# A new priority order in an attention and two-MLP kernel: the first weight group loaded ahead of the first values

## The chip, the cores and the metric

The kernel runs on one core of a Trainium2 chip. The metric is the time of one execution on the device in microseconds, median of the runs shown. Engines: PE (matrix products), DVE (vector), ACT (scalar and activation), POOL, and SP, which here only issues DMAs.

## The reference

Three steps follow one another on 2 images of 576 tokens, 8 heads of 64: attention, a first MLP, and a sum of four experts.

```python
scores = scale * np.matmul(q, k.transpose(0, 1, 3, 2))
mask_local = (rel >= 0) & (rel < stride)               # heads 0 to 3
mask_strided = (rel >= 0) & (pos[None, :] % stride == pos[:, None] % stride)   # heads 4 to 7
scores = np.where(masks[None, :, :, :], scores, -1000000000.0)
attn = softmax(scores)                                 # row maximum taken away
x = (attn @ v), heads side by side                     # 1152 x 512
h = np.maximum(np.maximum(x @ w1, x @ w2), x @ w3)     # 512 -> 768
x = h @ w_out                                          # 768 -> 512
p = domain_probs / (domain_probs.sum(-1, keepdims=True) + 1e-09)
for e in range(4):
    out += p[:, e:e + 1] * (np.maximum(x @ w1[e], 0.0) @ w2[e])   # 512 -> 1024 -> 512
```

The weights of the first MLP arrive as 64-bit floats, all else as 32-bit.

## The kernel before

Tokens are worked on in four parts i = 0 to 3: image i // 2, and in it the first 256 tokens (i even) or the last 320 (i odd). Heads go in four pairs p: 0 and 1 are the local ones, 2 and 3 the strided ones. Matrix products behind the attention use two 16-bit halves of each operand (a high and a low part, three products each), so every operand is scaled by a power of two and split: ACT writes the high half, DVE the low half (`split`, L135 to L137).

The attention and the first MLP are written as small steps ("atoms"), named by two letters and one or two digits; the string `ORDER` (L37) lists them, and the loop at L634 emits them one after another. The emission order is a priority: the framework (`schedule_with_timeline_sim`, L853) lays out a fixed order for each engine in advance from it, from data dependencies and free buffers, with times of its own. On the chip each engine then runs its list in that order. A wait of one instruction therefore holds what stands behind it on that engine.

The atoms:

- `lq i p` (L202) loads queries and keys of a part and pair, `lv i kind` (L208) its values (kind 0 local, 1 strided); `lw g` (L357) loads weight group g of the first MLP (one sixth of its hidden columns, all three matrices), `lo` (L429) half of its output matrix. All are DMAs issued by SP. Weight groups and output halves alternate between two landing buffers (`st64`, L66).
- `aa i p` (L233): scores on PE (a mask product at L259, then L264), row maximum on DVE (L268), its negative on DVE or POOL, exponentials with row sums on ACT (L275). `an` (L287): division by the sum on POOL and DVE. `at` (L300): transposes on PE (L310), copy on ACT (L312). `ap` (L315): product with the values (L337), then the scaled split into x (L344 on ACT, L345 on DVE).
- `vs i` (L222): scale of the values: two absolute maxima on DVE (L132), a maximum over partitions by a product on PE (L98, "rows") and a DVE reduction (L100), then small DVE steps to a power of two and its reciprocal (L105). Every scale goes through this chain (`scale_of`, `scale_of64`).
- `wd g` (L156): decoding of 64-bit words: two steps on ACT (L162, L163), two on DVE (L166, L167); the second writes tile r, of which there is one buffer (`RB`). `wa g` (L363): scale of a group, and `wp g` (L376): its split. `wa` has two branches: if the group is not yet decoded it takes a maximum over the raw words on DVE, else a sum of absolute values over the decoded ones on ACT (L129).
- `g i g'` (L382, digits part and group): 36 products into three PSUM tiles, combined by ACT, DVE and POOL (L396 to L400). `go i c` (L405): the second product of the first MLP, evicted by ACT (L418).
- `oa`, `od`, `os`, `op`: the same preparation for the output matrix. `fo` closes the attention's buffers and `cl` those of the first MLP.
- `ew`, `fw` (one step each of `prep_w1(0)`, L503, and `prep_w2(0)`, L533): the first expert's weights: a load, eight sums on ACT (L129), a scale, then splits; 17 steps of `ew` in all, of which the 11th to 17th are splits. `xw`, `yw` (`x2_ops`, L459): operands of the first expert's input for even and odd parts, 8 steps each. `m` (`gemm1(0, 0)`, L553): one of four blocks of the first expert's first product, seven products each, summed by DVE (L572 to L579).

The experts follow in a loop (L714). After each block of products a "slot" runs some steps of the next weights' preparation; `XS`, `W20`, `W10`, `W2S` and `W1S` (L31 to L35) say how many.

Of the kernel before, what the change touches and what calls it, by code (L numbers as in the profile page):

```python
# [27 lines left out]
ARS = 'pppd'  # L28
RB = 1
QB = 3  # L30
XS = [0, 0, 2]  # L31
W20 = [0, 1, 1, 2, 1, 5, 1, 2]
W10 = [4, 1, 2, 2, 5, 0, 4, 0]
W2S = [0, 1, 0, 0, 1, 1, 4, 4, 3, 0, 7, 5, 7, 3, 0, 3, 1]
W1S = [9, 3, 1, 2, 0, 13, 6, 6, 4, 0, 4, 4, 0, 6, 0, 4, 2]  # L35

ORDER = """  # L37
    lq00 aa00 lv01 lq03 lv00 lq01 aa01 vs0 an00 lq02 at00 ap00 lq20 aa02 lv21 lw0 an01 at01 ap01 an02 at02
    ap02 lw1 lq22 aa03 an03 at03 wa0 lq21 lq23 wd0 ap03 lv20 aa20 vs2 wa1 lq10 aa21 wd1 wp0 an20 at20 ap20
    lq12 lw3 an21 at21 aa22 g00 aa23 ap21 wp1 an22 lw2 lv11 at22 ap22 g01 wa2 an23 at23 lv10 lq11 ap23 wd2 wa3  # L40
    wd3 wp3 aa11 wp2 g20 lq32 g21 lv30 g03 aa10 an11 aa12 g23 vs1 lw4 at11 ap11 an10 at10 ap10 wa4 wd4 g02 wp4
    lq13 an12 lq30 g04 lv31 aa13 at12 ap12 lw5 wa5 an13 at13 lo0 lq31 wd5 lq33 wp5 aa30 ap13 g22 aa33 aa31 vs3
    lo1 an30 g24 at30 ap30 an31 at31 an33 ap31 at33 ap33 g25 aa32 an32 at32 ap32 oa0 od0 oa1 od1 os fo op0 ew
    g05 op1 op2 g10 op3 ew op4 ew op5 ew go20 ew go00 ew go23 ew g11 ew go22 ew g12 ew go21 ew go01 ew ew go03
    ew go02 g13 ew xw ew fw xw xw g14 ew g15 xw xw xw xw g30 g31 xw xw g32 g34 fw fw g33 fw fw g35 cl go10 m
    fw go13 m go30 fw go11 go12 fw go31 go32 go33 m yw m yw yw yw yw yw yw yw yw
"""
TINY = 2.0**-100
REBIAS = 2.0**-112
# [4 lines left out]
def kernel(ctx, tc, qk0l, qk0s, qk1l, qk1s, vl, vs0, vs1, vn, masks, w123, wo, probs, we1, we2, out):  # L54
# [652 lines left out]
    def step(gen, n=1):  # L707
        for _ in range(n):
            if gen is not None:
                next(gen, None)  # L710
# [3 lines left out]
    for e in range(E):  # L714
# [4 lines left out]
        def slot(k):  # L719
            nonlocal early  # L720
            if e == 0 and k < 8:
                step(gens["w2"], XS[k - 4] if k < 7 else 40)
            if k < 8 and e:
                step(w2g[e - 1], W2S[k] if k < 7 else 40)
            elif more:
                step(w2g[e], (W20 if k < 8 else W2S)[k])
            if more:
                n = 40 if k == 16 else W10[k] if e == 0 and k < 8 else W1S[k]
                if k < 8:
# [127 lines left out]
```

## Time and profile before

| | |
|---|---|
| time, median of 3 runs | 584.34 us (583.85 to 585.56) |
| the profiled execution's own time | 585.75 us |
| its span, first to last instruction | 584.0 us |
| mean granted TensorE clock | 0.974 |
| PE busy | 555.5 us (95%) |
| DVE busy | 367.5 us (63%) |
| ACT busy | 262.4 us (45%) |
| POOL busy | 125.9 us (22%) |
| DMA moved | 44.33 MB |

Shares over the whole span hide that the stages differ: the attention and the first weights lie in the first sixth or so, the experts in the last 350 us. The table of 40 slices and the table by stage are to be read first. PE's granted clock is a share of its full 2.4 GHz; the other level is half of it, and a number between is a mean over a stretch.

### The profile page before, as it was taken

Reading aid. Unit: us, or ns where it says so; the run is one execution under the profiler, and the core shown is the slowest. Engines: PE = TensorE matmul, PEld = TensorE weight load, DVE = VectorE, ACT = ScalarE, POOL = GpSimd, SP = SyncE. Lnnn points to the kernel's source line nnn. Section 1 sums busy time; section 2 is a strip of 40 time slices with the busy share of each in tenths; the row PEclk is TensorE's granted clock in tenths of the full one; section 3 lists DMA queues with packets and bytes.
Section 4 is the critical chain, followed back from the end, with each engine's and each line's share of the span. In section 5 each row is a group of like instructions: output and inputs, shape, how many; then the busy total and the mean of one; then the engine's idle time right before and its main releaser. Section 6 shows DMA issues by size and latency. Waiting matters only on the chain.

```text
span 584.0 us, 9782 instructions
## 1 busy us (share of the span) xinstructions
PE 555.5 (95%) x3943; PEld 375.7 (64%) x3943; DVE 367.5 (63%) x677; ACT 262.4 (45%) x557; POOL 125.9 (22%) x115
## 2 busy tenths in 40 slices
PE   7787889999799999999999999999999999999997
PEld 5576668888677777765445875445876445876443
DVE  4889799763773253888774865893765943765111
ACT  3868679573662122638654533523443520443000
POOL 1234344320212101012424221250221200221000
PEclk9679889999999999999999999999999999999999
DMA  8997355200040002203161000151000000000111
GB/s 274 389 304 253 142 192 192 88 2 1 2 145 0 1 2 74 73 1 121 36 230 47 1 2 1 39 184 65 2 1 1 1 0 1 1 2 0 55 54 55
DMA packets 16109, 44.33 MB, mean 76 GB/s; under 512 B 2280, under 2 KB 2280, under 8 KB 15296
## 3 DMA queue, kind: packets, MB, share of 16 engines
q1 hardware_dynamic: 15920, 43.41, 22.0%
q8 instruction: 31, 0.51, 0.4%
q10 hardware_dynamic: 144, 0.30, 0.2%
q14 instruction: 14, 0.11, 0.1%
HBM read 41.34 MB, written 2.36 MB: 75 GB/s over the span
## 4 chain that ended last, share of the span: by engine, by line
PE 82%; DVE 6%; ACT 4%; DMA 4%; issue 2%; POOL 1%; SPq 0%; DVEq 0%; ACTq 0%
PE e L350 11%; PE e L352 11%; PE e L351 10%; PE w L564 8%; PE w L566 8%; PE w L565 8%; PE g L350 7%; PE g L351 7%; PE g L352 7%; DMA v<-in_vs_dram 3%; PE ops L337 1%; PE sps L264 1%; DMA qk<-in_qk0l_dram 1%; ACT w1ops L136 1%; DVE r L167 1%
## 5 line engine op out<-in xcount | busy, mean ns | idle before, releaser
L565 PE MATMUL w<-xops,w1ops 128*128 128x256 f16 (+1 forms) x448 | 128.0, 286 | 0.7 <-DVE xops L473 0.7
L564 PE MATMUL w<-xops,w1ops 128*128 128x256 f16 (+1 forms) x448 | 127.6, 286 | 1.0 <-DVE c L573 0.6
L566 PE MATMUL w<-xops,w1ops 128*128 128x256 f16 (+1 forms) x448 | 128.0, 286 | 0.0
L350 PE MATMUL g<-x,w 128*128 128x256 f16 (+1 forms) x288 | 83.1, 291 | 4.2 <-ACT t L396 2.9
L351 PE MATMUL g<-x,w 128*128 128x256 f16 (+1 forms) x288 | 83.8, 292 | 0.0
L352 PE MATMUL g<-x,w 128*128 128x256 f16 (+1 forms) x288 | 83.0, 290 | 0.0
L586 POOL TENSOR_TENSOR h<-c,h 128x640 f16<-128x640 f32 (+1 forms) x28 | 36.5, 1303 | 185.6 <-ACT h L585 181.3
L694 DVE SCALAR_TENSOR_TENSOR x2acc<-e,coef,x2acc 128x512 f32<-128x512 f32 x27 | 20.1, 747 | 69.5 <-PE e L352 69.5
L588 ACT ACTIVATE h<-c 128x512 f16<-128x512 f32 (+1 forms) x36 | 24.1, 676 | 83.4 <-DVE c L578 83.2
L352 PE MATMUL e<-w,h 128*128 128x512 f16 x144 | 54.6, 379 | 0.0
L350 PE MATMUL e<-st,h 128*128 128x512 f16 x144 | 54.6, 379 | 0.0
L351 PE MATMUL e<-st,h 128*128 128x512 f16 x144 | 54.6, 379 | 0.0
L352 PE MATMUL e<-st,h 128*128 128x512 f16 x144 | 54.6, 379 | 0.0
L351 PE MATMUL e<-w,h 128*128 128x512 f16 x144 | 54.4, 379 | 0.0
L350 PE MATMUL e<-w,h 128*128 128x512 f16 x144 | 54.0, 379 | 0.0
L565 PEld LDWEIGHTS <-w1ops 128*128 128x128 f16 x448 | 43.8, 98 | 13.4 <-issue 1.6
L566 PEld LDWEIGHTS <-w1ops 128*128 128x128 f16 x448 | 43.8, 98 | 12.6 <-issue 1.7
L564 PEld LDWEIGHTS <-w1ops 128*128 128x128 f16 x448 | 43.8, 98 | 11.9 <-DVE c L577 0.2
L352 PEld LDWEIGHTS <-h 128*128 128x128 f16 x288 | 28.2, 98 | 34.0
L350 PEld LDWEIGHTS <-h 128*128 128x128 f16 x288 | 28.2, 98 | 33.0
L351 PEld LDWEIGHTS <-h 128*128 128x128 f16 x288 | 28.2, 98 | 32.7
L400 POOL TENSOR_TENSOR h<-t,h 128x256 f16<-128x256 f32 (+1 forms) x24 | 24.9, 1040 | 96.8 <-ACT h L399 96.8
(128 smaller groups left out, 1029.0 us busy)
## 6 DMA issues: line engine op xcount, KB each, us to landing
st<-in_we_dram SPq DMA_DIRECT2D x16, 1024.0 KB, 5.4
st<-in_w_dram SPq DMA_DIRECT2D x6, 1536.0 KB, 12.1
st<-in_wo_dram SPq DMA_DIRECT2D x2, 1536.0 KB, 6.4
qk<-in_qk1s_dram SPq DMA_DIRECT2D x4, 684.0 KB, 11.2
out_dram<-x2acc SPq DMA_DIRECT2D x8, 256.0 KB, 2.0
qk<-in_qk1l_dram SPq DMA_DIRECT2D x4, 496.0 KB, 11.4
qk<-in_qk0l_dram SPq DMA_DIRECT2D x4, 400.0 KB, 7.5
qk<-in_qk0s_dram SPq DMA_DIRECT2D x4, 384.0 KB, 11.1
```

Source lines behind the costliest of these rows:

```text
L136: nc.scalar.activation(hi, src, AF.Copy, scale=s)
L167: nc.vector.scalar_tensor_tensor(ri, gi, 3, lw, ALU.logical_shift_left, ALU.bitwise_or)
L350: nc.tensor.matmul(psum, lh, rh, start=i == 0, stop=False)
L351: nc.tensor.matmul(psum, lh, rl, start=False, stop=False)
L352: nc.tensor.matmul(psum, ll, rh, start=False, stop=i == n - 1)
L400: nc.gpsimd.tensor_tensor(hh[:, 1, fc, :], t1[:, :n], hh[:, 0, fc, :], ALU.subtract)
L564: nc.tensor.matmul(pt, wh, xh, start=k == 0, stop=False)
L565: nc.tensor.matmul(pt, wh, xl, start=False, stop=False)
L566: nc.tensor.matmul(pt, wl, xh, start=False, stop=k == 1)
L586: nc.gpsimd.tensor_tensor(lo, c[:, b], hi, ALU.subtract)
L588: nc.scalar.activation(hi, c[:, b], AF.Relu)
L694: nc.vector.scalar_tensor_tensor(acc[:, t, :], pt, coef[:, t : t + 1], acc[:, t, :], ALU.mult, ALU.add)
```

## The change

The atoms and their number stay the same; their order changes, and the slot counts with it. At the start `lq02` comes first and `lw0` ahead of `lv01`, `lq03` and `lv00`; `wa0`, `wd0` and `wp0` (scale, decoding and split of group 0) come ahead of the divisions, transposes and value products of part 0; `wa1` and `wd1` come behind part 0 and the first scores of part 2. `wd2` now stands ahead of `wa2`. Later on, `oa1` and `op3` are moved ahead of `oa0` and `op0`, the steps `ew`, `fw`, `xw` are dealt out anew among the `go` and `g1` blocks (the 15th to 17th `ew` now stand behind `g14`, `g33` and two more `xw`), and the last `m` stands behind eight `yw` in place of one.

```diff
--- before.py
+++ after.py
@@ -28,22 +28,22 @@
 ARS = 'pppd'
 RB = 1
 QB = 3
-XS = [0, 0, 2]
-W20 = [0, 1, 1, 2, 1, 5, 1, 2]
-W10 = [4, 1, 2, 2, 5, 0, 4, 0]
-W2S = [0, 1, 0, 0, 1, 1, 4, 4, 3, 0, 7, 5, 7, 3, 0, 3, 1]
-W1S = [9, 3, 1, 2, 0, 13, 6, 6, 4, 0, 4, 4, 0, 6, 0, 4, 2]
+XS = [0, 1, 1]
+W20 = [2, 1, 3, 2, 0, 5, 1, 2]
+W10 = [1, 1, 2, 2, 4, 4, 0, 3]
+W2S = [0, 0, 1, 0, 1, 1, 4, 6, 3, 0, 7, 5, 7, 3, 1, 3, 1]
+W1S = [8, 3, 1, 2, 0, 14, 6, 6, 4, 0, 4, 4, 0, 5, 0, 3, 3]
 
 ORDER = """
-    lq00 aa00 lv01 lq03 lv00 lq01 aa01 vs0 an00 lq02 at00 ap00 lq20 aa02 lv21 lw0 an01 at01 ap01 an02 at02
-    ap02 lw1 lq22 aa03 an03 at03 wa0 lq21 lq23 wd0 ap03 lv20 aa20 vs2 wa1 lq10 aa21 wd1 wp0 an20 at20 ap20
-    lq12 lw3 an21 at21 aa22 g00 aa23 ap21 wp1 an22 lw2 lv11 at22 ap22 g01 wa2 an23 at23 lv10 lq11 ap23 wd2 wa3
-    wd3 wp3 aa11 wp2 g20 lq32 g21 lv30 g03 aa10 an11 aa12 g23 vs1 lw4 at11 ap11 an10 at10 ap10 wa4 wd4 g02 wp4
-    lq13 an12 lq30 g04 lv31 aa13 at12 ap12 lw5 wa5 an13 at13 lo0 lq31 wd5 lq33 wp5 aa30 ap13 g22 aa33 aa31 vs3
-    lo1 an30 g24 at30 ap30 an31 at31 an33 ap31 at33 ap33 g25 aa32 an32 at32 ap32 oa0 od0 oa1 od1 os fo op0 ew
-    g05 op1 op2 g10 op3 ew op4 ew op5 ew go20 ew go00 ew go23 ew g11 ew go22 ew g12 ew go21 ew go01 ew ew go03
-    ew go02 g13 ew xw ew fw xw xw g14 ew g15 xw xw xw xw g30 g31 xw xw g32 g34 fw fw g33 fw fw g35 cl go10 m
-    fw go13 m go30 fw go11 go12 fw go31 go32 go33 m yw m yw yw yw yw yw yw yw yw
+    lq02 lq00 lq01 aa00 lw0 lv01 lq03 lv00 aa01 vs0 wa0 wd0 an00 lq20 at00 ap00 lw1 aa02 lv21 wp0 an01 at01
+    ap01 an02 lq22 aa03 an03 at02 lv20 ap02 at03 lq21 lq23 ap03 aa20 vs2 lq10 aa21 wa1 an20 at20 wd1 ap20 lq12
+    aa22 g00 lw3 an21 at21 aa23 ap21 wp1 an22 lw2 lv11 at22 ap22 an23 g01 at23 lv10 lq11 ap23 wd2 wa2 wa3 wd3
+    wp3 aa11 wp2 g20 lq32 g21 lv30 an11 g03 aa10 g23 aa12 vs1 lw4 at11 ap11 an10 at10 ap10 lq30 wa4 wd4 lq13
+    wp4 g04 g02 an12 lv31 aa13 at12 ap12 lw5 wa5 an13 at13 wd5 lq33 wp5 aa30 an30 ap13 lo0 lq31 aa33 aa31 vs3
+    g22 lo1 g24 at30 ap30 an31 at31 an33 oa1 at33 ap31 ap33 aa32 an32 oa0 at32 g25 od0 od1 ap32 os op3 op0 g10
+    op4 fo ew g05 op1 op2 ew ew op5 go20 ew go00 ew go23 ew ew g11 ew ew go22 ew g12 go21 ew go01 ew go03 ew
+    go02 ew xw g15 xw g13 fw g14 ew xw xw g30 g31 xw g32 xw fw g33 ew xw xw ew xw g34 fw fw fw g35 cl go10 m
+    go11 go30 fw m go13 fw go12 go31 go32 go33 m yw yw yw yw yw yw yw yw m yw fw
 """
 TINY = 2.0**-100
 REBIAS = 2.0**-112
```

## Rows read from the trace of the kernel before

**Rows 1.** Page, part 2: busy tenths in 40 slices of 14.6 us

```profile
PE   7787889999799999999999999999999999999997
DVE  4889799763773253888774865893765943765111
```

**Rows 2.** Busy us by stage: PE, PEld, DVE, ACT, POOL; clock, DMA share, GB/s

```profile
0.00:80.00 80.00, 60.55 (x496) 48.15 (x497) 61.80 (x116) 53.14 (x162) 25.08 (x40) 0.83 0.79 269
10.00:20.00 10.00, 9.06 (x57) 7.53 (x58) 7.05 (x23) 8.17 (x44) 3.83 (x9) 0.59 1.03 388
80.00:150.00 70.00, 70.00 (x705) 58.87 (x703) 50.20 (x98) 43.03 (x107) 17.77 (x23) 1.00 0.23 77
150.00:162.00 12.00, 8.78 (x65) 6.99 (x64) 10.78 (x11) 10.02 (x14) 4.48 (x3) 0.86 0.03 5
162.00:235.00 73.00, 73.00 (x558) 54.29 (x556) 29.47 (x63) 24.28 (x55) 9.19 (x10) 1.00 0.14 44
235.00:252.00 17.00, 15.43 (x123) 11.62 (x121) 16.88 (x39) 8.36 (x15) 0.00 (x0) 1.00 0.18 63
252.00:584.00 332.00, 327.79 (x2005) 195.77 (x2004) 198.35 (x355) 123.62 (x205) 69.34 (x40) 1.00 0.12 40
```

**Rows 3.** DMA issues, as in part 6 of the page: KB, us to landing

```profile
st<-in_w_dram SPq DMA_DIRECT2D x6, 1536.0 KB, 12.1
v<-in_vl_dram SPq DMA_DIRECT2D x2, 384.0 KB, 11.1
qk<-in_qk0l_dram SPq DMA_DIRECT2D x4, 400.0 KB, 7.5
qk<-in_qk0s_dram SPq DMA_DIRECT2D x4, 384.0 KB, 11.1
v<-in_vs_dram SPq DMA_DIRECT2D x2, 256.0 KB, 7.0
```

**Rows 4.** Instructions in order of time, start and us; values, group 0, part 0

```profile
9.58 1.22 DVE L132 TENSOR_REDUCE vm<-v 96x1 f32<-96x1024 f32 x1 [1.57 <-DMA v<-in_vl_dram]
...
10.97 0.34 ACT L275 ACTIVATE p<-sps,anm 128x96 f32<-128x96 f32 x1 [8.31 <-DVE anm L272]
...
13.71 0.15 DVE L105 RECIPROCAL s<-inv 128x1 f32<-128x1 f32 x1
...
18.10 1.72 DVE L132 TENSOR_REDUCE mx<-st 128x1 bf16<-128x1536 f32 x1
...
18.85 0.49 ACT L344 ACTIVATE x<-ops,s 128x256 f16<-128x256 f32 x1
...
37.59 0.45 DVE L345 SCALAR_TENSOR_TENSOR x<-ops,s,x 128x256 f16<-128x256 f32 x1
```

**Rows 5.** Instructions grouped by line and shape: busy us, mean ns, idle before

```profile
L132 DVE TENSOR_REDUCE mx<-st 128x1 bf16<-128x1536 f32 x6 | 10.4, 1741 | 1.1 <-DMA st<-in_w_dram 1.1
L166 DVE SCALAR_TENSOR_TENSOR st<-st 128x1536 int32<-128x1536 int32 x8 | 16.1, 2017 | 0.7 <-ACT st L163 0.4
L167 DVE SCALAR_TENSOR_TENSOR r<-st 128x1536 int32<-128x1536 int32 x6 | 11.2, 1864 | 0.0
L129 ACT ACTIVATE w1ops<-st 128x512 f16<-128x512 f32 x8 | 4.9, 614 | 0.0
```

**Rows 6.** Instructions in order of time, PE, its longest stall

```profile
31.52 0.29 PE L98 MATMUL rows<-identb,red 128*128 128x128 bf16 x1 [4.42 <-DVE red L95]
```

**Rows 7.** Instructions in order of time, DVE: group 2's maximum, scale, low half

```profile
43.02 1.75 DVE L132 TENSOR_REDUCE mx<-st 128x1 bf16<-128x1536 f32 x1 [1.11 <-DMA st<-in_w_dram]
...
61.09 0.15 DVE L105 RECIPROCAL s<-sinv 128x1 f32<-128x1 f32 x1
...
65.85 1.80 DVE L137 SCALAR_TENSOR_TENSOR w<-r,s,w 128x1536 f16<-128x1536 f32 x1
```

**Rows 8.** Instructions in order of time, ACT and PE, at 150 us

```profile
150.04 6.34 ACT L136 ACTIVATE w1ops<-st,s 128x1024 f16<-128x1024 f32 x6 [4.08 <-DVE s L105]
...
157.88 0.27 PE L350 MATMUL g<-h,wo_t 128*128 128x256 f16 x1 [3.22 <-ACT x2acc L418]
```

## The prediction

> **What bounds the kernel now.** I read the page's table of 40 slices first [rows 1]. The reader is to see two regimes in the PE line: sevens and eights in the first six slices (to about 88 us), then nines to the end, with a single seven in slice 11 (146 to 161 us) and the tail. DVE shows seven to nine tenths in slices 2 to 8 and falls off behind them. The table by stage [rows 2] puts numbers on it. From 0 to 80 us PE is busy for 60.55 us, so 19.45 us are idle, and DMA is busy 0.79 of the time; DVE works 61.80 us there. From 80 to 150 and from 162 to 235 us PE is never idle. Between them, from 150 to 162 us, it loses 3.22 us of idle time, and the granted clock averages 0.86, which over 12 us is another 1.7 us lost. From 235 to 252 us it loses 1.57 us with DVE busy for 16.88 of 17 us. After 252 us PE is idle for 4.2 us, nearly all of it the tail in which the last results are written out.
>
> So everything behind 80 us is PE work at full clock, in a queue. What the change makes of the end is decided by how much of that work is done, or startable, before 80 us, and by the two holes. A microsecond gained anywhere behind 80 us by an engine other than PE is worth nothing unless it closes a hole.
>
> **The moved load.** The change puts the load of weight group 0 (lw0) ahead of the first values (lv01, lv00) and of lq03, and lq02 ahead of everything. All of them are issues of SP; I take them to land in the order of issue. Sizes are in [rows 3]; in 10 to 20 us the queue moves 388 GB/s [rows 2]. Before, the first local values (lv00) end behind 400 + 256 + 384 + 384 KB and DVE's reduction over them starts at 9.58 us, on their arrival [rows 4]. After, 384 + 400 + 400 + 1536 + 256 + 384 KB are ahead of them: 3360 against 1040 KB, 2320 KB more, 6.1 us at 388 GB/s, so about 15.7 us. Group 0 itself has 1184 KB ahead of it in place of 2864 KB: 1680 KB less, 4.4 us, so its reduction can start at about 13.7 instead of 18.10 us [rows 4].
>
> What the late values cost: the scale of the values must be ready before the first x of image part 0 is written, at 18.85 us on ACT [rows 4]. From the reduction's start at 9.58 us to the end of the reciprocal at 13.86 us the chain took 4.3 us. At that length the scale is there at 20.0 us, and the first x comes 1.2 us later than before. What the early group gains: before, the four x of part 0 are complete at 38.04 us by the last line of [rows 4], and by then DVE has also spent the reduction and the two decoding steps of group 1, 1.74 + 2.02 + 1.86 = 5.6 us by their means [rows 5]. In the new order wa1 and wd1 stand behind the whole of part 0 (behind ap03, aa20, vs2). So x of part 0 can be complete 5.6 - 1.2 = 4.4 us earlier, with group 0 ready for it. PE's longest stall of all, 4.42 us before the row at 31.52 us, is a value-scale product that waits for a small DVE reduction [rows 6], queued among DVE's longer steps; with group 1's moved out of the way, part of it can go.
>
> But DVE's sum of work up to 80 us is the same: what moves ahead of part 0's end pushes group 1 behind it. PE wins only where it takes up a g1 block in time that it spent waiting. The bounds are +4.4 us (all of it reaches the end) and -6.1 us (the values' lateness passes to everything). I take +1.5 us, nearer to zero, because DVE is busy 61.80 of 80 us and most of its idle time lies before group 0 lands in either order.
>
> The added waits: DVE's reduction of group 0 waits for its DMA from before 13.7 us; behind it in DVE's order stand the small steps that free the exponentials (ACT sat 8.31 us in just this way before, for a DVE step behind the value reduction [rows 4]). The product for its scale waits on PE, with scores and transposes behind it. On ACT two decoding steps stand among the exponentials. These are in the lower bound.
>
> **Group 2's scale.** The new order has wd2 ahead of wa2. In the code scale_w then takes its other branch: the bound is a sum of absolute values on ACT over the decoded group, not a maximum on DVE over the raw one. DVE loses a reduction of 1.74 us [rows 5]. ACT gains three times the 0.614 us that a sum over 512 columns takes [rows 5], 1.8 us, in a stretch where it has room. The price is order: the scale can now start only when the group is decoded, and the decoded copy (tile r) has one buffer, which group 3 needs. Before, the chain from the maximum (done at 44.77 us) to the reciprocal (done at 61.24 us) took 16.5 us, nearly all of it queueing between longer DVE steps, and the low half was done at 67.65 us [rows 7]. If all of that chain now followed the decoding, group 3 would come some 7 us later; if it took the few small steps alone, nothing. Bounds -7 and +1.7 us; I take +1.0, since PE has two other groups to work on while the buffer is held.
>
> **The hole at 150 us.** ACT runs six scaled copies of the first expert's operand in one block, 6.34 us, and PE, whose results wait behind them to be evicted, sits for 3.22 us [rows 8]. In the new order four of these steps (the 11th to 14th ew) stand before the 15th, and the other three are moved behind g14, g33 and later ones. A block of four is 4.2 us instead of 6.34: the stall shrinks by 2.1 us, to 1.1 us. Bounds: +4.9 us (3.22 idle and the 1.7 us of low clock, all gone) and -3 us (the block keeps its length and meets another eviction, the same hole once more). I take +2.1.
>
> **The hole at 235 us.** The last m step now stands behind eight yw steps rather than one, so DVE writes the second operand set before the sums of the last block. PE waits there for either. DVE has no idle time to hide it in [rows 2], so one wait is traded for another: bounds +1.6 (all idle gone) and -2 us; I take +0.5.
>
> **The rest.** The other shifts in the order, the moved wo steps (op3, oa1) and the new slot counts (XS, W20, W10, W2S, W1S: one or two steps of operand preparation go to a neighbouring slot) lie beside a full PE, 327.79 of 332 us from 252 us on [rows 2]. That is their cover, so I cost them at nothing. If the cover goes, one step of about 1 us (6.34 over 6 [rows 8]) shows: -1 to +1 us.
>
> **The sum.** 1.5 + 1.0 + 2.1 + 0.5 + 0 = 5.1 us. The profiled execution took 585.75 us, of which 584.0 is the span; 580.65 us after. It lies 1.41 us above the median of the runs shown, 584.34 us, so the prediction for the median is 579.2 us.
>
> **The rivals.** *The clock stays up.* If the shorter gap at 150 us no longer lets the clock drop, its 1.7 us come back as well: 577.5 us. For it speaks that the low clock there follows the idle stretch directly; against it that a rest of 1.1 us remains. The Trainium skill, TensorE: Matmul & The Clock Gate, section "Why this matters for your kernels", advises against idle gaps between bursts of matmuls for this reason, and by that rule the term would be 3.8 us.
>
> *The late values decide (slower than before).* DVE's order puts a value reduction ahead of the small steps of the scores, so part 0 as a whole waits for lv00. Its price is the 6.1 us of lateness, less the 1.0 and the 2.1 + 0.5 of the other terms: 2.5 us slower, 586.8 us. For it: ACT's wait of 8.31 us was of this kind. Against it: 5.6 us of group 1 leave DVE before part 0 is done. It decides from the point where the last x of part 0 is written later than 38.04 us.
>
> *Nothing comes through.* DVE's sum is unchanged, the early gain is given back by 80 us, and the block on ACT re-forms elsewhere: only some of the holes is won, 583.5 us.
>
> *All comes through.* x of part 0 is 4.4 us earlier to the end, both holes go and DVE keeps the reduction: 4.4 + 1.7 + 4.9 + 1.6 = 12.6 us, 571.7 us.
>
> **How the numbers follow.** Chances: the forecast 0.35, the clock kept 0.15, late values 0.20, nothing 0.20, all 0.10. The deviations of the terms upward (2.9, 0.7, 2.8, 1.1, 1) make 4.4 us together if they are independent (root of the squares), downward (7.6, 8, 5.1, 2.5, 1) 12.5; the large downward ones are each unlikely. The range reaches to 573 and 589: it takes in the forecast, the clock, nothing and the late values with some room, and leaves out the full gain and the worst ends. About 0.3%, 1.75 us, is what a measurement of this kernel tells from no change. Faster than 582.6 us is nearly all of the forecast, the clock and the full gain, 0.60; within it 0.19, mostly "nothing"; slower 0.21, the late values and the tail of the forecast.
>
> **What would show it.** Right, step by step: the reduction of group 0 starts near 14 us and that of lv00 near 16; the last x of part 0 is written before 36 us; PE idle in 0 to 80 us falls from 19.45 to about 17; group 2 has one ACT sum and no DVE maximum, and its r is released by 68 us; PE idle in 150 to 162 us falls to about 1 us. Wrong: a stall of over 3 us on PE before 40 us behind a value or weight scale; r of group 2 held past 75 us; a block of five or more scaled copies on ACT with PE waiting; or PE idle that appears behind 252 us, where I have put nothing.

## The result, and the profile after

The changed kernel takes 577.34 us (median of 4 runs, 576.38 to 578.71) beside 584.95 us before (583.85 to 588.62 in the same comparison): ratio 0.9868, interval 0.9829 to 0.9908. Forecast were 579.2 us, range 573 to 589. The profiled execution takes 576.38 us with a span of 574.6 us, 9.4 us less span than before (584.0). The two medians lie only 7.6 us apart: the profiled execution is the fastest of the four after, and that of before lies above its median, so some 1.8 us of the 9.4 are scatter.

First the busy tenths of PE and DVE in 40 slices, part 2 of the page of the kernel after; they answer to [rows 1].

```profile
PE   5789699999999999899999999999999999999997
DVE  3888999687652254988864765984764943765111
```

The reader is to see that the seven in slice 11 is gone, and that DVE is at nine in slices 5, 6 and 7, where it had seven, nine and nine. The table by stage of the kernel after (busy us of PE, PEld, DVE, ACT, POOL; clock, DMA share, GB/s) answers to [rows 2]:

```profile
0.00:80.00 80.00, 63.20 (x543) 51.53 (x544) 64.61 (x125) 60.61 (x180) 29.45 (x42) 0.87 0.83 269
10.00:20.00 10.00, 4.86 (x20) 3.84 (x19) 6.75 (x11) 5.80 (x21) 2.80 (x6) 0.62 1.03 312
80.00:150.00 70.00, 69.50 (x703) 58.34 (x701) 57.50 (x102) 46.60 (x104) 20.21 (x24) 1.00 0.28 95
150.00:162.00 12.00, 11.78 (x92) 8.69 (x91) 6.19 (x16) 9.78 (x26) 0.80 (x1) 1.00 0.19 70
235.00:252.00 17.00, 15.37 (x108) 10.21 (x106) 15.45 (x30) 8.78 (x15) 2.52 (x2) 1.00 0.00 1
```

PE is busy for 63.20 us of the first 80, was 60.55, at a clock of 0.87, was 0.83. The hole at 150 us has shrunk from 3.22 to 0.22 us of idle time, and the clock there is 1.00. The hole at 235 us (1.63 us) is as it was (1.57).

I add up in this way. From a span I take the first 80 us, and what PE loses behind them: its idle time, and its busy time times (1 - granted clock) in windows of 2 us. What is left is the PE work at full clock that was still to be done at 80 us, "work left at 80" from here on; it tells what the order up to there has gained, whatever happens later.

| profiled execution | span | PE idle behind 80 us | lost to low clock behind 80 us | work left at 80 us |
|---|---|---|---|---|
| before | 584.0 | 9.01 | 1.74 | 493.25 |
| after | 574.6 | 6.47 | 0.00 | 488.13 |

So the 9.4 us are 5.1 us from the start of the kernel, and 4.3 us from less idle time and no low clock later: the hole at 150 us gives back 3.0 us of idle and 1.7 us of clock, and 0.5 us of new idle time comes up between 80 and 130 us. In the first 80 us the second half gave most. Here are the rows 0 to 40 and 40 to 80 us of the same view, first of before, then of after:

```profile
0.00:40.00 40.00, 29.63 (x216) 22.35 (x217) 27.45 (x63) 23.75 (x74) 9.47 (x20) 0.74 0.97 334
40.00:80.00 40.00, 30.91 (x287) 25.80 (x284) 34.35 (x53) 29.39 (x90) 15.61 (x20) 0.92 0.61 203
```

```profile
0.00:40.00 40.00, 30.02 (x214) 22.74 (x215) 27.06 (x63) 25.04 (x74) 10.56 (x21) 0.79 0.98 330
40.00:80.00 40.00, 33.18 (x331) 28.79 (x330) 37.55 (x63) 35.57 (x107) 18.89 (x22) 0.96 0.69 208
```

Busy time times clock: 29.63 x 0.74 = 21.9 and 23.7 us in the first 40 (1.8 us more), 28.4 and 31.9 us in the next 40 (3.4 us more). DVE works 0.4 us less in the first and 3.2 us more in the second.

The instructions of the start in the kernel after, in order of time (start, us, engine, line; in brackets the idle time before and what ended it), answer to [rows 4] and [rows 6]:

```profile
12.19 1.75 DVE L132 TENSOR_REDUCE mx<-st 128x1 bf16<-128x1536 f32 x1 [1.50 <-DMA st<-in_w_dram]
...
16.45 1.22 DVE L132 TENSOR_REDUCE vm<-v 96x1 f32<-96x1024 f32 x1 [1.23 <-DMA v<-in_vl_dram]
...
22.52 1.72 DVE L132 TENSOR_REDUCE mx<-st 128x1 bf16<-128x1536 f32 x1
...
25.41 0.15 DVE L105 RECIPROCAL s<-inv 128x1 f32<-128x1 f32 x1
...
27.77 1.73 DVE L166 SCALAR_TENSOR_TENSOR st<-st 128x1536 int32<-128x1536 int32 x1
...
33.45 1.75 DVE L167 SCALAR_TENSOR_TENSOR r<-st 128x1536 int32<-128x1536 int32 x1
...
43.12 0.45 DVE L345 SCALAR_TENSOR_TENSOR x<-ops,s,x 128x256 f16<-128x256 f32 x1
```

```profile
27.89 0.51 ACT L344 ACTIVATE x<-ops,s 128x256 f16<-128x256 f32 x1
```

```profile
15.14 4.11 PE L264 MATMUL sps<-qk 128*128 128x64 f32 x16 [3.28 <-DMA qk<-in_qk0s_dram]
...
29.62 0.29 PE L98 MATMUL rows<-identb,red 128*128 128x128 bf16 x1 [0.18 <-DVE red L95]
```

Group 0's reduction starts at 12.19 us (18.10 before), that of the first local values at 16.45 (9.58). The scale of the values comes 9.1 us behind that start, the first x is written at 27.89 (18.85), and the last x of part 0 is done at 43.57 us, 5.5 us later than before. The rows at 22.52, 27.77 and 33.45 us are the reduction and the two decoding steps of group 1: on DVE they still stand ahead of that last x, although `wa1` and `wd1` stand behind part 0 in `ORDER`. PE's 4.42 us stall of [rows 6] is down to 0.18 us, but PE now stands 3.28 us at 15 us for queries and keys that are loaded behind group 0. The weight groups went the other way; group 2 in the kernel after, for [rows 7] (ACT's row stands first):

```profile
48.06 1.48 ACT L129 ACTIVATE w<-r 128x1536 f16<-128x1536 f32 x1
```

```profile
44.88 1.74 DVE L167 SCALAR_TENSOR_TENSOR r<-st 128x1536 int32<-128x1536 int32 x1
...
58.94 1.92 DVE L137 SCALAR_TENSOR_TENSOR w<-r,s,w 128x1536 f16<-128x1536 f32 x1
```

Its low half starts at 58.94 us (65.85 before). Last the place of the former hole, ACT and PE of the kernel after, for [rows 8]:

```profile
133.93 0.42 ACT L396 COPY t<-g 128x320 f32<-128x320 f32 x1 [0.69 <-PE g L352]
134.89 6.34 ACT L136 ACTIVATE w1ops<-st,s 128x1024 f16<-128x1024 f32 x6 [0.53 <-DVE s L105]
141.14 0.45 ACT L418 ACTIVATE x2acc<-g,x2s 128x256 f32<-128x256 f32 x1
```

The block of scaled copies is still six long and still takes 6.34 us. It now waits 0.53 us for its scale (4.08 before) and stands directly behind the eviction of the first tile of a g1 block.

### The profile page after: what moved, and what is told of

It is laid out like the page before. It is cut to its first block, busy times and chain, and to the rows that moved or that the text cites. A ratio compares the mean times of both kernels' runs of the same rounds, so it can differ in the third digit from the quotient of the medians.

```text
span 574.6 us, 9788 instructions
## 1 busy us (share of the span) xinstructions
PE 551.3 (96%) x3944; PEld 373.6 (65%) x3944; DVE 364.6 (63%) x676; ACT 264.4 (46%) x559; POOL 127.9 (22%) x115
## 4 chain that ended last, share of the span: by engine, by line
PE 77%; DVE 8%; DMA 6%; ACT 5%; issue 3%; POOL 1%; SPq 0%; ACTq 0%; DVEq 0%; POOLq 0%
PE e L350 11%; PE e L352 11%; PE e L351 11%; PE w L564 9%; PE w L566 9%; PE w L565 8%; PE g L350 6%; PE g L351 6%; PE g L352 6%; DMA v<-in_vl_dram 2%; DMA st<-in_w_dram 2%; ACT w L129 1%; PE ops L337 1%; DMA st<-in_we_dram 1%; ACT p L275 1%
## 5 line engine op out<-in xcount | busy, mean ns | idle before, releaser
L351 PE MATMUL g<-x,w 128*128 128x256 f16 (+1 forms) x288 | 82.4, 288 | 0.0
L350 PE MATMUL g<-x,w 128*128 128x256 f16 (+1 forms) x288 | 81.6, 289 | 0.2 <-ACT t L396 0.2
L352 PE MATMUL g<-x,w 128*128 128x256 f16 (+1 forms) x288 | 81.8, 286 | 0.0
L400 POOL TENSOR_TENSOR h<-t,h 128x256 f16<-128x256 f32 (+1 forms) x24 | 21.9, 918 | 89.4 <-ACT h L399 89.4
```

Source lines behind the costliest of these rows:

```text
L350: nc.tensor.matmul(psum, lh, rh, start=i == 0, stop=False)
L351: nc.tensor.matmul(psum, lh, rl, start=False, stop=False)
L352: nc.tensor.matmul(psum, ll, rh, start=False, stop=i == n - 1)
L400: nc.gpsimd.tensor_tensor(hh[:, 1, fc, :], t1[:, :n], hh[:, 0, fc, :], ALU.subtract)
```

## The experiments

All times are beside the kernel before on the same chip; "hole" is the idle time of PE between 130 and 175 us.

| run | median, us (before beside it) | ratio, interval | hole | low clock, 130 to 200 | work left at 80 |
|---|---|---|---|---|---|
| after | 577.34 (584.95) | 0.9868 [0.9829, 0.9908] | 0.22 | 0.00 | 488.1 |
| e1_new_head | 584.51 (585.75) | 0.9970 [0.9943, 0.9997] | 6.38 | 1.66 | 487.5 |
| e2_new_tail | 582.44 (585.75) | 0.9945 [0.9915, 0.9974] | 2.03 | 1.60 | 492.2 |
| e3_slots | 584.95 (585.75) | 0.9993 [0.9963, 1.0023] | 3.22 | 1.41 | 495.4 |
| e4_lw0_only | 583.70 (585.75) | 0.9974 [0.9945, 1.0003] | 4.10 | 1.44 | 490.2 |
| e5_lw0_back | 593.93 (585.15) | 1.0115 [1.0055, 1.0176] | 5.76 | 2.51 | 495.9 |
| e6_wa2_first | 580.96 (585.15) | 0.9914 [0.9879, 0.9950] | 0.36 | 0.00 | 492.3 |
| e7_scale_back | 577.10 (585.15) | 0.9836 [0.9790, 0.9883] | 1.73 | 0.00 | 488.2 |
| e8_scale_fwd | 586.72 (585.15) | 1.0017 [0.9991, 1.0044] | 5.30 | 0.00 | 493.1 |
| e9_block_behind | 587.19 (585.66) | 1.0020 [0.9996, 1.0044] | 3.69 | 1.39 | 494.0 |
| e10_prep_back | 583.20 (585.66) | 0.9959 [0.9940, 0.9979] | 0.69 | 0.00 | 490.6 |
| e11_wd2_first | 588.64 (585.66) | 1.0054 [1.0021, 1.0087] | 4.77 | 1.35 | 491.2 |
| e12_block_before | 587.50 (585.56) | 1.0041 [1.0012, 1.0071] | 4.88 | 1.25 | 491.7 |

Work left at 80 comes from one profiled execution each. Six of these kernels (before, e2, e3, e8, e9, e12) have the same old order up to there: 491.7 to 495.4, mean 493.3. Three (after, e1, e7) have the new one: 487.5 to 488.2, mean 487.9. So the new start is worth 5.4 us by the means, and a single difference of less than some 2 us says nothing. Counted inside the first 80 us instead, in the same windows, idle time and low clock together make 29.3 us on average over the six and 25.2 us over the three. Of these 4.1 us, 3.7 are idle time (19.5 and 15.8 us) and 0.4 low clock (9.9 and 9.4 us); in the one pair of before and after it is 2.7 us idle time and 2.9 us clock. How much of a gain is clock can't be told from one pair.

### The two halves and the slots

e1 has the new order up to `os` and the old one behind it, with the old slots; e2 the reverse; e3 has only the new slots.

```diff
 # e1: ORDER, new up to ap32, old from os on
-    lq00 aa00 lv01 lq03 lv00 lq01 aa01 vs0 an00 lq02 at00 ap00 lq20 aa02 lv21 lw0 an01 at01 ap01 an02 at02
+    lq02 lq00 lq01 aa00 lw0 lv01 lq03 lv00 aa01 vs0 wa0 wd0 an00 lq20 at00 ap00 lw1 aa02 lv21 wp0 an01 at01
...
 # e3: ORDER as before
-W20 = [0, 1, 1, 2, 1, 5, 1, 2]
+W20 = [2, 1, 3, 2, 0, 5, 1, 2]
...
```

> The new order up to the atom os, the old order and slot counts behind it. Theory (two separate gains, 5.2 us from the order up to 80 us, 4.2 us from the hole at 150 us): ratio about 0.991, PE idle from 0 to 80 us near 16.8 us as with the whole change, and a PE stall of about 3 us behind a block of scaled copies on ACT still there near 145 us. Rival (the hole goes because the head shifts the timing): ratio about 0.987 and no stall above 1 us behind 80 us.

> The old order up to the atom os, the new order and slot counts behind it. Theory: ratio about 0.993, PE idle from 0 to 80 us 19.5 us as before, no PE stall above 1 us between 140 and 165 us. Rival (head shifts the timing): ratio about 1.000 and the stall of about 3 us stays.

> The old order with the new slot counts alone. Theory: ratio 1.000 within 0.002, since PE is full behind 252 us in both. Rival: the slot counts are part of the gain, ratio 0.997 or less, with PE idle behind 252 us below 4.2 us.

e1 starts as well as the whole change (487.5 us left) and then loses it at the old hole, with a second stall of 2.7 us behind it, which was not expected; so its ratio is 0.997 where 0.991 was expected. ACT's block and PE's stall in e1:

```profile
144.34 6.35 ACT L136 ACTIVATE w1ops<-st,s 128x1024 f16<-128x1024 f32 x6 [4.08 <-DVE s L105]
```

```profile
152.17 0.27 PE L350 MATMUL g<-h,wo_t 128*128 128x256 f16 x1 [3.22 <-ACT x2acc L418]
```

Same 4.08 us wait, same 3.22 us stall as in [rows 8]: the hole belongs to the order behind `os`, not to the start. e2 has the block as the kernel after has it (at 138.38 us, 0.53 us wait, no stall behind it) and the old start; a stall of 2.03 us comes up later, at 162 us. The two halves alone gave ratios of 0.3% and 0.55%, together 1.3%. The sum of the two is smaller, and each half alone has a stall that the whole change doesn't have (2.73 us in e1, 2.03 in e2); but with intervals of some 0.3% either way, that each needs the other is not shown. e3 moves nothing that can be measured.

### The parts of the start

e4 is the old order with `lw0` alone moved ahead of `lv01`. e5 is the new order with `lw0` behind `lv00`. e10 leaves `lw0` early in the new order and puts `wa0`, `wd0`, `wp0` back to where they stood.

```diff
 # e4, on the order before
-lq00 aa00 lv01 lq03 lv00 lq01 ... aa02 lv21 lw0 an01
+lq00 aa00 lw0 lv01 lq03 lv00 lq01 ... aa02 lv21 an01
 # e5, on the order after
-aa00 lw0 lv01 lq03 lv00 aa01
+aa00 lv01 lq03 lv00 lw0 aa01
 # e10, on the order after
-vs0 wa0 wd0 an00 ... lv21 wp0 an01 ... at03 lq21 lq23 ap03 ... wd1 ap20
+vs0 an00 ... lv21 an01 ... at03 wa0 lq21 lq23 wd0 ap03 ... wd1 wp0 ap20
```

> The old order with one atom moved: lw0 directly ahead of lv01. Theory (the early group is what gives the head's gain, by freeing its landing buffer for group 2 some 7 us earlier): ratio about 0.992, the load of group 2 issued near 23 us instead of 30.7 us. Rival (the load alone makes the values late and the rest of the new order is what repairs it): ratio 1.003 or more, the last x of part 0 later than 38 us.

> The whole change, but lw0 behind lv00 as in the old order; the early scale, decoding and split of group 0 and all else stay. Theory (the load ahead of the values is the cause of the head's gain of about 5 us): the PE work left at 80 us rises by 3 us or more against the whole change, ratio to before 0.993 or more. Rival (the priority of group 0's preparation and the later place of group 1 give it, the load's place does not matter): work left at 80 us within 1.5 us of the whole change, ratio about 0.987.

> The order after, with wa0, wd0 and wp0 put back to where they stood before among their neighbours (wa0 behind at03, wd0 behind lq23, wp0 behind wd1), the load lw0 left early. Theory: the early load pays because group 0 is decoded early and gives its landing buffer to group 2; with the decoding late, lw2 is issued late again, and the PE work left at 80 us goes from 488 back to between 490 and 493 us: 579 to 582 us. Rival: the place of the load in SP's queue is what counts, and the steps of preparation are ordered by their data anyway: 577 us, lw2 still issued near 23 us.

e4 starts 3.1 us better than the old order's mean and gives a part of it back at the hole (4.10 us in place of 3.22). Its time came out between the two sides, 0.9974 with an interval up to 1.0003, so it is not clearly faster than before. The third load of weights is issued at 18.02 us there, and the last x of part 0 is done at 46.33 us, so each side had its sign. But the low halves of groups 2 and 3 come at 66.59 and 77.50 us, much as before (65.85 and 78.45): a landing buffer that comes back early does not by itself bring these groups forward. e5 is the only version of the new order that is slower than before, by 1.2%: 8 us of the start are gone, 5.8 us of hole and 2.5 us of clock come on top, and 3.8 us of idle time and clock between 80 and 130 us. Its first 40 us in the table by stage:

```profile
0.00:40.00 40.00, 30.59 (x174) 22.32 (x175) 26.33 (x60) 23.72 (x73) 7.39 (x20) 0.66 0.98 330
```

PE is as busy as in the kernel after (30.02 us) but at 0.66 of its clock in place of 0.79. That is 4.1 us of clock (30.59 x 0.34 = 10.4 us against 30.02 x 0.21 = 6.3 us). Over all of the first 80 us, in windows of 2 us, e5 has 6.2 us more of low clock and 1.8 us more of idle time than the kernel after. The expectation did not have the clock. In e10 the third load of weights is still issued early, at 22.64 us (23.28 after, 30.66 before), as its rival said; but the low halves of groups 0 and 1 come at 33.88 and 43.55 us (31.06 and 38.64 after), those of groups 2 and 3 at 63.98 and 75.20 (58.94 and 71.63), and the time is 583.2 us. On DVE the reduction and the decoding of group 0 stayed early too (11.56, 17.02 and 19.42 us; 12.19, 17.98 and 20.57 after), so what the edit moved are the splits. The early load and decoding did not suffice with the splits later; whether the splits alone make the difference is not shown, as the planner moved other steps with them. A part of the loss lies behind 80 us: between 80 and 130 us PE is idle for 2.69 us (0.50 after). Of the theory the work left came true (490.6 us), its path (a late third load) not, and the time is somewhat over what it expected.

e6 is the new order with `wa2` ahead of `wd2` again, e11 the old order with `wd2` ahead of `wa2`.

```diff
 # e6, on the order after
-ap23 wd2 wa2 wa3 wd3
+ap23 wa2 wd2 wa3 wd3
 # e11, on the order before
-g01 wa2 an23 at23 lv10 lq11 ap23 wd2 wa3
+g01 an23 at23 lv10 lq11 ap23 wd2 wa2 wa3
```

> The whole change, but wa2 ahead of wd2 as in the old order, so that group 2's scale is a maximum over the raw words on DVE again. Theory (the sum on ACT is worth about 1 us): 1 us slower than the whole change, ratio to before 0.988 to 0.990. Rival (holding tile r for the later scale costs): up to 3 us faster than the whole change, ratio 0.982 to 0.986.

> The order before with one edit: wd2 ahead of wa2, so that group 2's scale is taken from a sum on ACT over the decoded group instead of a maximum on DVE over the raw one. Theory, from the run that put wa2 ahead in the order after and lost 3 to 4 us: the exchange is worth as much here, 581 us, with the low half of group 2 written some 4 us earlier than at 65.85 us. Rival: it pays only where group 2 has come early, as in the order after; here group 2 lands late and its chain is bounded by the landing buffer: 585 us, low half within 2 us of 65.85.

e6 loses 4 us of the start (492.3 left) and is 3.9 us slower than e7 beside it, whose program is that of the kernel after but for one step. Group 2 itself is not later there: its low half starts at 58.81 us (58.94 after). What is late is group 3. DVE in e6, in order of time:

```profile
63.74 1.75 DVE L167 SCALAR_TENSOR_TENSOR r<-st 128x1536 int32<-128x1536 int32 x1
...
75.58 1.76 DVE L132 TENSOR_REDUCE mx<-st 128x1 bf16<-128x1536 f32 x1 [2.23 <-DMA st<-in_w_dram]
...
78.68 2.05 DVE L137 SCALAR_TENSOR_TENSOR w<-r,s,w 128x1536 f16<-128x1536 f32 x1 [0.37 <-ACT w L136]
```

The maximum of a later group stands ahead of group 3's low half in DVE's list and waits 2.23 us for its data; in the kernel after it stands behind it (71.63, then 75.10 us). But what DVE's low half waits for last is ACT, whose high half of group 3 comes at 77.10 us (67.72 after). ACT and PE in e6:

```profile
75.58 1.62 ACT L162 ACTIVATE st<-st 128x1536 int32<-128x1536 uint16 x1 [2.99 <-DMA st<-in_w_dram]
77.10 1.55 ACT L136 ACTIVATE w<-r,s 128x1536 f16<-128x1536 f32 x1
78.56 0.34 ACT L396 COPY t<-g 128x256 f32<-128x256 f32 x1
```

```profile
78.95 0.37 PE L350 MATMUL g<-x,w 128*128 128x256 f16 x1 [2.61 <-ACT t L396]
```

In ACT's list a decoding step of the later group stands in front and waits 2.99 us for the same data; behind the high half stands an L396, and PE stands 2.61 us for it. The kernel before has the same stall, there because ACT waits for tile r of group 3:

```profile
74.11 1.58 ACT L136 ACTIVATE w<-r,s 128x1536 f16<-128x1536 f32 x1 [2.90 <-DVE r L167]
75.60 0.35 ACT L396 COPY t<-g 128x256 f32<-128x256 f32 x1
```

```profile
76.00 0.27 PE L350 MATMUL g<-x,w 128*128 128x256 f16 x1 [2.62 <-ACT t L396]
```

In the kernel after, group 3's high half is through by 69.3 us, and PE has no stall of more than 0.3 us between 70 and 80 us. So the exchange of `wa2` and `wd2` changed the planner's order on both engines, and its worth is not the 1.74 us reduction that DVE is spared. That this stall is the whole price of e6 is not shown: up to 80 us PE is idle for less time there than in the kernel after (14.3 and 16.8 us) and loses more to low clock (13.9 and 8.0 us). In e11, where group 2 has not come early, the same exchange makes group 2 later, 71.30 us for the low half (65.85 before), and the kernel 0.5% slower. The rival expected no such delay, and its reason is not what the trace shows: group 2 is decoded earlier than before (r is complete at 53.02 us, 56.45 before), but its scale now follows the decoding and is there at 66.1 us (61.24 before). So e11 is worse than either side expected, and the exchange has no price of its own. Its start is no worse by the work left (491.2 us); the loss lies behind 80 us, with 1.0 us of idle time and 3.0 us of low clock between 80 and 130 us and a larger hole.

### The hole at 150 us

e7 puts the step with the scale (the tenth `ew`) later in the new order, e8 puts it earlier in the old one, e9 puts it earlier still, e12 deals the steps so that the block comes first of all.

```diff
 # e7, on the order after
-ew ew go22 ew g12 go21
+ew ew go22 g12 ew go21
 # e8, on the order before
-go22 ew g12 ew go21
+go22 ew ew g12 go21
 # e9, on the order before
-g11 ew go22 ew g12 ew go21
+g11 ew ew ew go22 g12 go21
 # e12, on the order before
-op3 ew op4 ew op5 ew go20 ew go00 ew go23 ew g11 ew go22 ew g12 ew go21
+ew ew ew op3 op4 op5 ew ew ew ew ew go20 go00 go23 ew g11 go22 g12 go21
```

> The whole change, but the tenth ew (the scale of the first expert's weights) behind g12 again instead of ahead of it; nothing else. Theory (the hole at 150 us is ACT waiting in its order for this scale, whose product stands on PE behind the 36 products of g12, and then running its six copies): the wait of ACT for the reciprocal grows from 0.53 us to 3 us or more, PE stalls about 3 us behind the block and the clock drops after it; 3 to 5 us slower than the whole change, ratio to before about 0.993. Rival (the hole went because the other ew, xw and go were dealt out anew): no stall above 1 us, ratio as with the whole change, 0.987.

> The old order and slot counts, with the tenth ew moved ahead of g12; nothing else. Theory: the wait of ACT for the reciprocal falls from 4.08 us to about 0.5 us, the stall of 3.22 us and the 1.7 us of low clock behind it go, ratio to before about 0.992. Rival (re-dealing of the rest decides): the stall of 3 us stays, ratio 1.000.

e7 tells nothing on the hole: the planner left the block in the same place, with the same 0.53 us wait, and the time is that of the kernel after (its 1.73 us in the table are another stall, at 158 us). e8 takes the wait away, and the hole stays. ACT and PE in e8:

```profile
143.75 0.47 ACT L418 ACTIVATE x2acc<-g,x2s 128x256 f32<-128x256 f32 x1 [4.80 <-PE g L352]
144.97 6.35 ACT L136 ACTIVATE w1ops<-st,s 128x1024 f16<-128x1024 f32 x6 [0.75 <-DVE s L105]
151.22 0.41 ACT L396 COPY t<-g 128x320 f32<-128x320 f32 x1
```

```profile
151.68 0.27 PE L350 MATMUL g<-h,wo_t 128*128 128x256 f16 x1 [3.02 <-ACT t L396]
```

The block has moved ahead of the L396 that stood in front of it. PE fills its three tiles with the g1 block and stands until that L396 frees one. So taking the wait away is not enough, and a second theory was formed: it is the place of the block.

> The order before with two of the steps `ew` (the scale among them) moved ahead of go22 and g12, so that the scale is there earlier and ACT's block of six scaled copies stands directly behind the eviction of the first tile of a g1 (L396) and ahead of a g2 eviction (L418), as in the order after; the start of the kernel, up to 80 us, is untouched. Theory, formed on the run in which the wait alone was taken away: the hole depends on what stands on either side of the 6.34 us block, not on the wait for the scale and not on the length of the block. While the block runs, PE has the other two tiles of that g1, which DVE frees, and one or two more. Then PE idle in 130 to 175 us falls from 3.22 to below 0.7 us, the clock there stays at 1.00, the block is still about 6.3 us long, and the time is the one before less 3.22 + 1.70 us: about 580 us. Rival: ACT's in-order queue meets a full PE wherever a block of 6.3 us stands, so a stall of 2 to 3 us comes back behind another eviction, as in the run with the scale moved alone: 583 to 586 us.

It fell as well. ACT and PE in e9:

```profile
139.69 0.42 ACT L396 COPY t<-g 128x320 f32<-128x320 f32 x1 [1.16 <-PE g L352]
144.25 6.35 ACT L136 ACTIVATE w1ops<-st,s 128x1024 f16<-128x1024 f32 x6 [4.13 <-DVE s L105]
150.50 0.45 ACT L418 ACTIVATE x2acc<-g,x2s 128x256 f32<-128x256 f32 x1
```

```profile
151.00 0.43 PE L350 MATMUL g<-x,w 128*128 128x320 f16 x1 [2.81 <-ACT x2acc L418]
```

The block stands where it should, directly behind L396, but the edit did not bring the scale earlier: the wait is 4.13 us, and PE stands 2.81 us. In the kernel before, the two evictions on either side of the block were, on ACT:

```profile
145.54 0.43 ACT L396 COPY t<-g 128x320 f32<-128x320 f32 x1 [1.21 <-PE g L352]
...
157.36 1.19 ACT L418 ACTIVATE x2acc<-g,x2s 128x256 f32<-128x256 f32 x3
```

With these runs the arithmetic closes to about 0.3 us. It is the time between two evictions on ACT against the work that PE can put into its three tiles meanwhile. Behind an L396, DVE frees the other two tiles of that g1 block, so PE has five tiles ahead of it: two of 1.63 us (12 products at 0.136 us), then a g2 tile of 1.96 us and two more of 1.63, with a scale product of 0.22: 8.7 us (9.4 us in the kernel before, where all three new ones are g2 tiles). Behind an L418 that empties the tiles it has three tiles: those of the next g1 block, 4.9 us, or in e5 two g2 tiles and one of g1 with a scale product, 5.8 us.

| run | ACT ahead of the block | wait for the scale | ACT behind it | from one to the other | PE stall |
|---|---|---|---|---|---|
| before, e1, e3, e11 | L396 | 4.08 | three L399, L418 | 11.8 | 3.22 |
| e9 | L396 | 4.13 | L418 | 10.8 | 2.81 |
| e4, e8 | L418 | 0.74, 0.75 | L396 | 7.5 | 3.02 |
| e5 | L418, L399 | 0.57 | L418 | 10.1 | 4.59 |
| after, e2, e6, e7, e10 | L396 | 0.53 | L418 | 7.2 | 0 |

The times run from the start of one eviction to the start of the other; PE goes on about 0.5 us behind the second. So the sums are 11.8 + 0.5 - 9.4 = 2.9 us for before, 2.6 for e9, 3.1 for e8 and 4.8 for e5, beside the stalls of the last column. Only with the block behind an L396 and the scale in time are 7.2 us set against 8.7 us of work. The kernel before had the right place and lacked the scale: by this sum some 3.5 us less of waiting would have closed its hole. No run shows that alone, as e8 took the wait away and the planner gave up the place with it. e12 was made to try this arithmetic beforehand: the scale in time, the block ahead of the whole g1 block.

> The order before with the steps `ew` dealt out so that the product for the scale stands on PE directly behind three g2 tiles and ACT's block of six copies ahead of all three tiles of the g1 that follows (ACT: three L418, the block, L396); the start up to 80 us is untouched. Theory, from the five runs so far: the stall is the time from one eviction on ACT to the next, less what PE can do meanwhile in its three result tiles, plus the tiles that DVE frees, which stand behind the next L396. From rows of before: the third g2 tile ends near 136.9, the scale follows the product by 1.5 us (148.54 to 150.04), so the block starts near 138.5 with a short wait of about 1 us, and ends 6.25 us later, near 144.8; L396 ends near 145.2. PE has three tiles of 12 products at 0.136 us, 1.63 us each, from 137.1: it stands from about 142.0 to 145.2. Expected: a stall of about 3.2 us on PE that ends with L396, though the wait for the scale is gone; total time within 2 us of the one before. Rival: the wait of 4.1 us for the scale is what makes the hole; with it gone the stall falls under 1 us and the time to 580 to 582 us.

ACT and PE in e12:

```profile
136.78 6.34 ACT L136 ACTIVATE w1ops<-st,s 128x1024 f16<-128x1024 f32 x6 [0.74 <-DVE s L105]
143.03 0.40 ACT L396 COPY t<-g 128x320 f32<-128x320 f32 x1
```

```profile
143.49 0.37 PE L350 MATMUL g<-h,wo_t 128*128 128x256 f16 x1 [3.02 <-ACT t L396]
```

Expected were 3.2 us behind L396, measured 3.02, with a wait of 0.74 us for the scale. A further stall of 1.87 us came at 159 us, where three L399 and an L418 stand behind eight sums that wait for weights; that one was not expected. The kernel is 0.4% slower than before.

## Why the prediction was right or wrong

**The time** lies in the range and 1.9 us under the forecast, but not by the path that I gave, and its closeness is partly luck: in the profiled pair both main terms came out at about twice their size, and the step that was to carry the first did not happen. The profiled execution gained 9.4 us where the sum had 5.1: the two terms of the start were 2.5 us and gave 5.1, the hole was 2.1 and gave 4.7, the 235 us hole was 0.5 and gave nothing, and 0.5 us of idle time between 80 and 130 us was not in the sum. The idle time up to 80 us fell to 16.8 us, as I had said (about 17); the rest of the 5.1 us is, in this pair, a higher granted clock there (0.87, was 0.83), for which I had no term.

**The moved load** can't be sized by itself; with the term of group 2 it gave 5.1 us, inside their bounds together (up to +6.1). The step that was to bring it about failed. Group 0 and the late values came near where I put them (12.19 against 13.7 us, 16.45 against 15.7). Then I took the scale's chain at its old length of 4.3 us and x of part 0 to be complete 4.4 us earlier, before 36 us, because 5.6 us of group 1 would leave DVE before that. The chain took 9.1 us, since two decoding steps and two reductions of 1.2 to 1.75 us stand between its small ones on DVE, the first x came 9.0 us later (1.2 in my sum), and the last x of part 0 was done at 43.57 us, 5.5 us later. Group 1 did not leave DVE: its reduction and decoding, 5.2 us, still ran ahead of that x, and a decoding step of group 2 with them (41.18 us). I had read `ORDER`, and what counts is the order that the planner made of it. The 4.42 us stall did go, as I thought it might, but 3.28 us came back at 15 us, behind queries and keys that the load pushed back; this price I had not named. What pays shows behind 40 us: the landing buffer of group 0 is given back 7 us earlier (third load issued at 23.28 us, 30.66 before), groups 2 and 3 are split 7 us earlier (58.94 and 71.63; 65.85 and 78.45 before), and PE, with g1 blocks to fall back on, does 3.4 us more work between 40 and 80 us. That path is read from one trace; e4, where the buffer comes back still earlier and the groups do not, shows that the first of these does not bring the second by itself. I had written that DVE's sum up to 80 us is the same; it is 64.61 in place of 61.80 us. That the load's place carries the gain in the new order is shown by e5 (8 us more work left, 1.2% slower than before). e4 and e10 move the work left by 3 and 2.4 us, little more than the scatter, though e10's time is clearly above that of the kernel after (0.9959 and 0.9868, intervals apart). How the 5 us divide between the parts stays open: they don't add up, as each moves the planner's order for the others.

**Group 2's scale.** That the branch changes, with one ACT sum and r released at 60.9 us (before 68), was right. The reasons were not: r is held for 16.0 us in place of 13.7, and DVE's 1.74 us are not what counts. In the new order the exchange is worth some 4 us (e6), and what the traces show for it is a stall of PE of 2.6 us behind group 3's high half on ACT; in the old one alone it does harm (e11). The upper bound of 1.7 us left out that the planner orders everything anew.

**The hole at 150 us.** The stall went, close to its upper bound of 4.9 us, but not by a shorter block: it kept six copies and 6.34 us. The prediction listed what stood on ACT and its length; it did not ask what PE could do meanwhile, which is 8.7 or 4.9 us by the place of the block, nor why ACT had waited 4.08 us ahead of it. The place of the four `ew` in `ORDER` did not set the block's length: the planner put six copies together again. e8, e9 and e12 show that either condition alone, the place or the scale in time, gives nothing; both together stand in the kernel after, e2, e6, e7 and e10, and none of them has a stall at the block.

**The clock** rival gave 577.5 us and the measurement is 577.3, but by a different sum: the whole hole went, so its condition, a rest of 1.1 us, never came to be tried; that the numbers agree is luck. The Trainium skill, TensorE: Matmul & The Clock Gate, section "Why this matters for your kernels", warns against such gaps. The traces agree in part: behind stalls of 3.02 us the clock fell to 0.54 in e4 and 0.50 in e12 (both in 144 to 146 us), and in e8 it stayed at 1.00; behind a stall of 2.03 us in e2 it fell to 0.50 (164 to 166 us), behind one of 1.73 us in e7 it stayed at 1.00.

**The late values** rival named the point from which it decides: x of part 0 later than 38.04 us. It was 43.57 us, and the kernel is faster. The point was wrong, since PE does not need part 0 complete while other scores and groups are there to work on.

**The 235 us hole and the rest.** The one wait was traded for the other exactly (1.65 us of idle time in 232 to 260 us before, 1.64 after). Idle time behind 252 us is 4.1 us (4.2 before), so nothing came up there. The slots are worth nothing that e3 can measure (0.9993, interval 0.9963 to 1.0023).

## What to carry to other kernels

A long block on the engine that evicts results is harmless if the time between the evictions on either side of it is shorter than the work that fits into the result tiles in between: count both, with the wait ahead of the block, before costing it by its length. Where a planner fixes the order of each engine, an edit of one priority has no price of its own: read the order that comes out, on every engine, before arguing from the order that was written. And a late operand need not cost anything while the bounding engine has other work that is ready; ask what becomes ready earlier, not only what becomes late.

## What the runs showed of the hardware

The start of this kernel scatters more than the rest. In six kernels with the same order up to 80 us PE lost 4.3 to 9.2 us to the low clock in the first 40 us, and was idle for 10.2 to 12.8 us; the two together make 17.0 to 20.2 us. The clock rises and falls at other moments although the order is the same: between 12 and 18 us it is 0.50 in the kernel before and 1.00 in e12. A stall of 3.02 us behind the same two steps of ACT (the block of copies, then L396) was followed by a low clock in e4 and e12 and by none in e8; what tells these apart was not found.
